# A mean's matmuls in a PSUM bank of their own, beside an open accumulation group (threshold attention and a feed-forward block, fp32)

## The chip, the cores and the metric

The kernel runs on one core of a Trainium2 chip. The metric is the device time of one execution in microseconds (us); the time before is the median of three runs, 1344.65 us (1344.35 to 1345.46). The profile is of one further execution. In it PE is TensorE's matmuls and PEld its weight loads, DVE is VectorE, ACT is ScalarE, POOL is GpSimd and SP the engine that issues most DMAs. Times inside the profile count from the start of its span.

## The reference

```python
# q, k, v: (8, 8, 576, 64) fp32; tau scalar
scores = scale * np.matmul(q, k.transpose(0, 1, 3, 2))
thresh = np.max(scores, axis=-1, keepdims=True) - tau
scores = np.where(scores >= thresh, scores, -1000000000.0)
attn = softmax(scores)                       # exp of scores - max, over its sum
x = matmul(attn, v), heads side by side      # (8, 576, 512)
mu = np.mean(x, axis=-1, keepdims=True)
var = np.mean((x - mu) ** 2, axis=-1, keepdims=True)
xn = (x - mu) / np.sqrt(var + 1e-06) * g_ln
out = x + np.maximum(xn @ w_ch1, 0.0) @ w_ch2   # w_ch1 (512, 2048), w_ch2 (2048, 512)
```

Softmax is written out in the reference; it is shortened here. All matrix work is in fp32.

## The kernel before

**Two streams.** The attention part goes through 72 steps, nine for each of the 8 batches (`SLOTS`). In a step PE makes scores, DVE takes the maxima, ACT the exponentials (L432), DVE the threshold and the sum (L439), POOL the division (L455); the weights are turned by DVE and two DMAs, and PE multiplies them with the values (L598, L608). The feed-forward part works on 16 groups of 288 tokens, two for each batch. `x` is held with features on the partitions, four slices of 128 features by 288 tokens.

**Order.** The order of the instructions on each engine is written out by hand (`manual_schedule`). Each step has four quarters. The feed-forward part of a group is a generator (`ffn_steps`): each `yield` hands back a kind and a cost, and `second_part` (L1035) lets it issue so many products in a quarter as a budget allows (`owed`). So PE's queue is a mixture of both streams, in a fixed order. A product (L96) is two matmuls of 64 output partitions each, and each of them stands in the trace as two weight loads and two matmuls, so a product is four of each.

**A group.** `mean_of` (L681) multiplies the sums over the four slices (`sums`, made by POOL at L650) with a constant matrix of 1/512 (`average`, L662), which leaves each token's mean on all partitions, tokens of the first half on partitions 0 to 63 and of the second on 64 to 127. `spread` then copies it with four ACT instructions (L674) into a tile in SBUF. `centre` (L691) subtracts it from the four slices of `x` with four DVE instructions (L698), which gives `xc`. `first_part` (L800) multiplies `xc` with w_ch1: 16 tiles of four products, each with a PSUM bank `p1`, emptied by ACT with the ReLU (L829). `second_quarters` (L871) multiplies the result with w_ch2 in seven segments of 16 products of 144 columns, instead of eight, with sums and differences of the weights prepared ahead (s2, s3, s4) and of the hidden values made on the way. Each segment (L903) accumulates in one PSUM bank `seg`, and ACT copies it out (L922). The seventh, with the weights s4 (kept in the tile `e`), is `p3`; the one before it is `p5`. The last group ends with `last_tiles` in place of the seventh segment.

**Banks.** Six of the eight PSUM banks hold scores. Two are left for all else (pool `ps_ff`, tag "ff", `bufs=2`): `p1`, `seg`, `mean` and, in the first steps, other tiles take them in turn. The framework orders engines by bank: an instruction that writes a bank waits until an instruction of another engine that was given that bank ahead of it is through, also where they touch other columns.

**The mean among the segments.** While the seven segments of a group are under way (`banks_taken`, L961), a mean that falls due for the next group is put on a list (`waiting_mean`). The seventh segment takes it up when its index d reaches 4 (`mean_from`): the mean is then put into columns 288 to 431 of the segment's own bank, with `start=False`, since the segment has opened the bank. A mean that falls due later than that, or while no segments run, takes a bank of its own (`start=True`). `centre` has to wait for the mean, and `first_part` of the next group for `xc`.

Of the kernel before, what the change touches and what calls it, by code (L numbers as in the profile page):

```python
# [8 lines left out]
F32 = mybir.dt.float32  # L9
# [9 lines left out]
def kernel(  # L19
# [41 lines left out]
    TOK = S // 2  # L61
# [14 lines left out]
    ps_ff = ctx.enter_context(tc.tile_pool(name="ps_ff", bufs=2, space=bass.MemoryType.PSUM))  # L76
# [19 lines left out]
    def product(out, lhsT, rhs, **flags):  # L96


        for h in range(2):
            r = slice(64 * h, 64 * h + 64)  # L100
            nc.tensor.matmul(out[r], lhsT=lhsT[:, r], rhs=rhs, **flags)  # L101
# [25 lines left out]
    def load_v(u):  # L127
# [21 lines left out]
        out=tau_sb, in_=bass.AP(tensor=tau.tensor, offset=tau.offset, ap=[[0, 128], [1, 1]])  # L149
# [5 lines left out]
    for t in v_rest:  # L155
# [9 lines left out]
        out=scl_sb, in0=tau_sb, scalar1=0.0, scalar2=SCALE, op0=ALU.is_ge, op1=ALU.mult  # L165
    )
    nc.vector.tensor_scalar(
        out=low_sb, in0=tau_sb, scalar1=0.0, scalar2=BIG, op0=ALU.is_lt, op1=ALU.mult
    )
    nc.vector.scalar_tensor_tensor(  # L170
        out=low_sb, in0=tau_sb, scalar=-1.0, in1=low_sb, op0=ALU.mult, op1=ALU.subtract
# [393 lines left out]
    groups, sums = {}, {}  # L565
# [89 lines left out]
    means, centred = {}, {}  # L655

    waiting_mean, banks_taken, among = [], [False], []

    HT = TOK // 2
    early, late = slice(0, HT), slice(HT, TOK)  # L660

    def average(to, bank, rhs, start, bias=None):  # L662


        for h in range(2):
            nc.tensor.matmul(
                bank[64 * h : 64 * h + 64], lhsT=avg_sb[:, 64 * h : 64 * h + 64],
                rhs=rhs[:, (early, late)[h]], start=start, stop=True, skip_group_check=True,
            )

        def spread():
            for at in range(2):
                for h in range(2):
                    nc.scalar.activation(  # L674
                        to[64 * at : 64 * at + 64, (early, late)[h]], bank[64 * h : 64 * h + 64],
                        func=AF.Identity, **({"bias": bias[64 * h : 64 * h + 64]} if bias is not None else {}),
                    )

        return spread

    def mean_of(g, bank=None):  # L681
        if bank is None and banks_taken[0]:
            waiting_mean.append(g)
            return
        start = bank is None
        if start:
            bank = ps_ff.tile([128, HT], F32, tag="ff", name="mean")
        means[g] = ffn.tile([128, TOK], F32, tag="mean", bufs=1, name="mean")
        average(means[g], bank, sums.pop(g), start)()

    def centre(g):  # L691
        nonlocal issued
# [14 lines left out]
    def drip(room=None, everything=False):  # L707


        urgent = [i for i, d in enumerate(drops) if d[0]]  # L710
        n = urgent[-1] + 1 if urgent else 0
        room = dict(room or {})
        while drops:
            _, when, eng, cost, go = drops[0]
            if n <= 0 and not everything:
                if when == now or room.get(eng, 0) < cost:
                    break
                room[eng] -= cost
            drops.pop(0)
            n -= 1  # L720
            go()
# [6 lines left out]
    def run_all(calls):  # L728
        now = calls[:]
        calls.clear()  # L730
        for fn in now:
            fn()
# [6 lines left out]
    def store(eng, g, m, o):  # L739
        ot = ffn.tile([128, TOK], F32, tag="o", bufs=4, name="ot")  # L740
        eng.transpose(ot, o)
        stores.append(lambda: send(g, m, ot))
# [27 lines left out]
    HD, HM = ND // 2, NK // 2  # L770
# [100 lines left out]
    def second_quarters(g, rb):  # L871
# [4 lines left out]
        s2, s3, s4 = more  # L876
        b11, b12 = hidden[:, :HD, early], hidden[:, :HD, late]
        b21, b22 = hidden[:, HD:, early], hidden[:, HD:, late]
# [21 lines left out]
                at = (slice(None), slice(d, d + 4))  # L900
                eng.tensor_tensor(out=out[at], in0=in0[at], in1=in1[at], op=op)  # L901

        def segment(weights, rhs, out=None, mean_from=HD):  # L903
            whole = ps_ff.tile([128, 512], F32, tag="ff", name="seg")
            bank = whole[:, :TOK].rearrange("p (m t) -> p m t", m=HM)
            for d in range(HD):
                if d == mean_from:
                    banks_taken[0] = False
                    while waiting_mean:
                        mean_of(waiting_mean.pop(0), whole[:, TOK : TOK + HT])  # L910
                        yield 2, 0
                for m in range(HM):
                    at, end = (d, m), (HD - 1, HM - 1)
                    product(
                        bank[:, m], lhsT=weights[:, m, d], rhs=rhs[:, d],
                        start=at == (0, 0), stop=at == end,
                    )
                    if at != end:
                        yield 2, 0.5
            if out is None:  # L920
                out = ffn.tile([128, HM, HT], F32, tag="part", bufs=4, name="part")
            nc.scalar.copy(out, bank)  # L922
            return out

        def last_tiles(weights, rhs):


            for m in range(HM):
                bank = ps_ff.tile([128, HT], F32, tag="ff", name="end")
                for d in range(HD):  # L930
                    product(
                        bank, lhsT=weights[:, m, d], rhs=rhs[:, d],
                        start=d == 0, stop=d == HD - 1,
                    )
                    if d < HD - 1:
                        yield 2, 0.5
                drip(everything=True)
                z = ffn.tile([128, HT], F32, tag="part", bufs=4, name="z")
                dve.tensor_tensor(out=z, in0=bank, in1=rb[:, late], op=ALU.mult)
                add(dve, y12[:, m], y12[:, m], z)  # L940
                store(dve, g, m, y[:, m])
                run_all(stores)
                if m < HM - 1:
                    yield 2, 0.5

        def add(eng, out, a, b):
            eng.tensor_tensor(out=out, in0=a, in1=b, op=ALU.add)
# [11 lines left out]
        ends_here = g == NG - 1  # L959
        later(("t3", 3, by_fours, pool, b12, b22, b12, ALU.subtract), urgent=pool)  # L960
        banks_taken[0] = True  # L961
        yield from segment(w2[0, 0], b11, y11)
        need("t3")
        later(("t2", 3, by_fours, dve, b11, b11, b12, ALU.add), urgent=dve)
        yield 2, 0.5
        p2 = yield from segment(w2[0, 1], b21)
        need("t2")
        later(("t4", 3, by_fours, pool, b21, b21, b11, ALU.subtract), urgent=pool)
        yield 2, 0.5
        p7 = yield from segment(s3, b12)  # L970
        yield 2, 0.5
        yield from segment(s2, b11, y12)
# [20 lines left out]
        else:  # L993
            later(("hi", 3, finish, pool, 1))
        yield 2, 0.5
        p3 = yield from last_tiles(s4, b22) if ends_here else segment(s4, b22, None, 4)
        if not ends_here:
            later(
                ("12", 1, add, dve, y12, y12, p3), ("done12", 2, finish, pool, 0, 1),
# [35 lines left out]
    def second_part(n, i):  # L1035

        nonlocal issued, owed, part, now
        part, now = i, QUARTERS * n + i
        if not queue:
            return  # L1040
        at = QUARTERS * n + i
        g = sum(issued >= e for e in ends)
        left = sum(ROOM[t % QUARTERS] for t in range(at, ready(g + 1))) if g + 1 < NG else 0
        owed += (ends[g] - issued) * ROOM[i] / left if left > 0 else 8


        steps = 0
        got = 1 if i in (0, QUARTERS - 1) else 2
        while queue and (owed >= 0.5 or got == 1 and i in (0, QUARTERS - 1)):
            got, cost = next(queue[0], (None, 0))  # L1050
            if got is None:
                queue.pop(0)
                got = 1
            elif got == 0:
                owed = 0.0
                break
            else:
                issued += cost
                owed -= cost
                steps += 1  # L1060
                if steps == 4 and among:
                    mean_of(among[0])
                    centre(among.pop())

    def group_ready(g):
        first = divmod(ready(g), QUARTERS)
        before = divmod(ready(g) - 1, QUARTERS) if g else first
        if g == 1:
            at_quarter(*before, lambda: among.append(g))
        else:  # L1070
            at_quarter(*before, mean_of, g)
            at_quarter(*(first if g and first[1] else before), centre, g)
        at_quarter(*first, lambda: queue.append(ffn_steps(g)))
# [4 lines left out]
    else:  # L1078
# [3 lines left out]
        for i in range(ND):  # L1082
            nc.sync.dma_start(
                out=w2_sb[:, :, i],
# [181 lines left out]
```

## Time and profile before

| what | value |
|---|---|
| median of 3 runs | 1344.65 us (1344.35 to 1345.46) |
| the profiled execution | 1344.68 us |
| its span, first to last instruction | 1342.9 us |
| granted TensorE clock, mean | 0.998 |
| chain that ended last, share of PE | 87% (DVE, ACT and POOL 3% each) |
| mean spreads at L674 (ACT), one instruction | 28 from a `seg` bank, median 285 ns; 36 from a `mean` bank, 284 ns |
| copy of a segment at L922 (ACT) | 399 ns |
| one `xc` subtraction at L698 (DVE) | median 451 ns |

A line of the groups reads: line, engine, operation, out<-in, partitions x elements, count; then busy time and mean ns of one; then the time that the engine stood idle just before them, and what ended most of it. A line of the timeline reads: start, duration, engine, line, operation, out<-in, count, and in brackets the idle time before it and what ended that. Matmuls overlap, so their own lengths are longer than the beat at which they follow each other: matmuls of 144 columns last 286 ns each and their pairs follow each other every 122 ns.

### The profile page before, as it was taken

Reading aid. Unit: us, or ns where it says so; the run is one execution under the profiler, and the core shown is the slowest. Engines: PE = TensorE matmul, PEld = TensorE weight load, DVE = VectorE, ACT = ScalarE, POOL = GpSimd, SP = SyncE. Lnnn points to the kernel's source line nnn. Section 1 sums busy time; section 2 is a strip of 40 time slices with the busy share of each in tenths; the row PEclk is TensorE's granted clock in tenths of the full one; section 3 lists DMA queues with packets and bytes.
Section 4 is the critical chain, followed back from the end, with each engine's and each line's share of the span. In section 5 each row is a group of like instructions: output and inputs, shape, how many; then the busy total and the mean of one; then the engine's idle time right before and its main releaser. Section 6 shows DMA issues by size and latency. Waiting matters only on the chain.

```text
span 1342.9 us, 40339 instructions
## 1 busy us (share of the span) xinstructions
PE 1305.7 (97%) x17304; PEld 985.6 (73%) x17304; DVE 874.0 (65%) x1544; ACT 490.7 (37%) x1107; POOL 628.1 (47%) x836
## 2 busy tenths in 40 slices
PE   8899899999999999999999999999999999999997
PEld 7665457769686786868778696877869687786957
DVE  7879886667666775666756677656766667665113
ACT  5866333242424333242333324233232323334130
POOL 3565556535445444444535454443444445344312
PEclk9999999999999999999999999999999999999999
DMA  8937874557643775447644576447764376444211
GB/s 167 295 102 183 204 187 156 178 155 195 176 150 120 194 203 158 151 156 191 174 151 151 165 179 191 143 143 192 194 178 152 120 197 185 129 152 133 85 19 20
DMA packets 335299, 213.93 MB, mean 159 GB/s; under 512 B 247376, under 2 KB 292688, under 8 KB 327056
## 3 DMA queue, kind: packets, MB, share of 16 engines
q1 hardware_dynamic: 329008, 210.46, 54.7%
q8 instruction: 136, 2.23, 0.7%
q10 hardware_dynamic: 5952, 0.74, 0.4%
q0 software_dynamic: 160, 0.15, 0.1%
q14 instruction: 43, 0.35, 0.1%
HBM read 124.00 MB, written 87.29 MB: 157 GB/s over the span
## 4 chain that ended last, share of the span: by engine, by line
PE 87%; DVE 3%; ACT 3%; POOL 3%; DMA 1%; issue 1%; SPq 1%; POOLq 0%; DVEq 0%; ACTq 0%
PE p L101 35%; PE seg L101 30%; PE sc L405 10%; PE sc L598 8%; PE sc L608 2%; DVE e L439 1%; ACT e L432 1%; POOL w L308 1%; ACT mean L674 1%; PE tp L101 1%; POOL e L455 1%; DMA qk_room<-in_k_dram 1%; SPq L118 1%; POOL hidden L844 0%; ACT em L489 0%
## 5 line engine op out<-in xcount | busy, mean ns | idle before, releaser
L101 PE MATMUL p<-xc,w 128*64 128x288 f32 x4096 | 519.8, 407 | 1.4 <-DVE xc L698 1.1
L101 PEld LDWEIGHTS p<-xc,w 128*64 128x64 f32 x4096 | 287.1, 137 | 204.8 <-issue 13.9
L419 DVE TENSOR_REDUCE neg<-sc 128x2 f32<-128x1152 f32 x144 | 188.9, 1352 | 256.6 <-PE sc L405 255.4
L455 POOL TENSOR_SCALAR e<-e,den 128x576 f32<-128x576 f32 x264 | 211.8, 814 | 133.6 <-DVE den L444 133.6
L101 PE MATMUL seg<-hidden,w 128*64 128x144 f32 x3840 | 247.9, 287 | 0.0
L101 PEld LDWEIGHTS seg<-hidden,w 128*64 128x64 f32 x3840 | 234.9, 137 | 11.5 <-issue 8.6
L439 DVE SCALAR_TENSOR_TENSOR e<-sc,thr,e 128x576 f32<-128x576 f32 x288 | 222.5, 810 | 20.2 <-POOL thr L423 11.6
L423 POOL TENSOR_SCALAR thr<-neg,low_sb 128x2 f32<-128x2 f32 x144 | 39.4, 274 | 378.8 <-DVE neg L419 376.4
L829 ACT ACTIVATE hidden<-p 128x288 f32<-128x288 f32 x256 | 106.4, 416 | 282.6 <-PE p L101 280.6
L432 ACT ACTIVATE e<-sc,neg 128x576 f32<-128x576 f32 x288 | 197.6, 753 | 2.6 <-DVE neg L419 2.5
L529 DVE STREAM_TRANSPOSE et<-e 128x1152 f32<-128x1152 f32 x118 | 161.1, 1372 | 14.5 <-POOL e L455 14.0
L405 PE MATMUL sc<-kT,qT 64*64 64x384 f32 (+3 forms) x2048 | 140.3, 403 | 2.8 <-DVE e L439 2.1
L598 PE MATMUL sc<-em,v_in 128*64 128x128 f32 (+1 forms) x2368 | 130.1, 263 | 2.7 <-DVE w L300 1.3
L598 PEld LDWEIGHTS sc<-em,v_in 128*64 128x64 f32 x2368 | 122.8, 137 | 11.6 <-DVE w L300 1.5
L101 PE MATMUL seg<-hidden,stage 128*64 128x144 f32 x1920 | 123.3, 286 | 0.0
L621 ACT COPY x<-sc 128x128 f32<-128x128 f32 x120 | 31.6, 266 | 245.7 <-PE sc L405 176.7
L101 PEld LDWEIGHTS seg<-hidden,stage 128*64 128x64 f32 x1920 | 117.6, 137 | 2.9 <-issue 2.9
L405 PEld LDWEIGHTS sc<-kT,qT 64*64 64x64 f32 x2048 | 76.3, 133 | 44.4 <-issue 21.4
L901 POOL TENSOR_TENSOR hidden<-hidden 128x576 f32<-128x576 f32 x60 | 84.8, 1428 | 50.7 <-ACT hidden L829 40.9
L922 ACT COPY part<-seg 128x288 f32<-128x288 f32 x74 | 29.9, 405 | 162.3 <-PE seg L101 162.1
L901 DVE TENSOR_TENSOR hidden<-hidden 128x576 f32<-128x576 f32 x60 | 50.3, 873 | 47.2 <-PE seg L101 44.2
L101 PE MATMUL seg<-hidden,e 128*64 128x144 f32 x896 | 60.4, 287 | 9.1 <-ACT mean L674 9.1
(134 smaller groups left out, 1069.5 us busy)
## 6 DMA issues: line engine op xcount, KB each, us to landing
scr<-et SPq DMA_DIRECT2D x63, 1152.0 KB, 5.0
em<-scr SPq DMA_DIRECT2D x63, 1024.0 KB, 5.7
out_dram<-ot SPq DMA_DIRECT2D x248, 36.0 KB, 3.7
q_in<-in_q_dram SPq DMA_DIRECT2D x120, 72.0 KB, 2.8
er<-scr SPq DMA_DIRECT2D x132, 64.0 KB, 5.2
k_in<-in_k_dram SPq DMA_DIRECT2D x116, 72.0 KB, 3.0
v_in<-in_v_dram SPq DMA_DIRECT2D x28, 256.0 KB, 5.4
w<-in_moe_w_ch_dram SPq DMA_DIRECT2D x10, 512.0 KB, 7.9
```

Of the source, the lines that this page charges most:

```text
L101: nc.tensor.matmul(out[r], lhsT=lhsT[:, r], rhs=rhs, **flags)
L405: nc.tensor.matmul(sc[h][64 * i : 64 * i + 64, at : at + n], lhsT=ql[r] if s == HP else qT[r, half, j * 128 + 64 * i : j * 128 + 64 * i + 64],
L419: nc.vector.tensor_reduce(out=neg[:, i], in_=pairs[h], axis=AXL.X, op=ALU.max, negate=True,)
L423: nc.gpsimd.tensor_scalar(out=thr[:, i], in0=neg[:, i], scalar1=-1.0, scalar2=low_sb, op0=ALU.mult, op1=ALU.add,)
L432: nc.scalar.activation(es[:, i], blocks[i], func=AF.Exp, bias=neg[:, i : i + 1])
L439: nc.vector.scalar_tensor_tensor(out=es[:, i], in0=blocks[i], scalar=thr[:, i : i + 1], in1=es[:, i], op0=ALU.is_ge, op1=ALU.mult, accum_o ...
L455: nc.gpsimd.tensor_scalar(out=es[:, i], in0=es[:, i], scalar1=den[:, i : i + 1], scalar2=1.0, op0=ALU.mult, op1=ALU.mult,)
L529: nc.vector.transpose(et[:, :, 64 * h : 64 * h + 64].rearrange("p n (j c) -> p j n c", j=2), es[:, 2 * h : 2 * h + 2].rearrange("p j (n c) ...
L598: nc.tensor.matmul(dst[64 * h : 64 * h + 64], lhsT=vt[:, h, c, :], rhs=pick(em[:, 2 * j : 2 * j + 2, c], h), start=c == 0 and first, stop= ...
L621: nc.scalar.copy(x_of(2 * b + (s > HP))[:, s % (HP + 1), 128 * j : 128 * j + 128], pv[j])
L829: nc.scalar.activation(hidden[:, d], p1, func=AF.Relu)
L901: eng.tensor_tensor(out=out[at], in0=in0[at], in1=in1[at], op=op)
```

## The change

The argument `mean_from` goes, and with it the mean inside the segment: a segment's bank holds the segment alone. The seventh segment is now stepped from outside. After eight of its steps the list of waiting means is worked off, and each mean takes a bank of its own, as the others do. After it a tile `passed` is taken from the same pool, which nothing writes or reads. Then the segment goes on. The words that come with the change say: "A group's mean in a bank of its own, four products sooner; the turn of the two free banks moved on by one, so that the next group's first tile takes it".

```diff
-    def mean_of(g, bank=None):
-        if bank is None and banks_taken[0]:
+    def mean_of(g):
+        if banks_taken[0]:
             waiting_mean.append(g)
             return
-        start = bank is None
-        if start:
-            bank = ps_ff.tile([128, HT], F32, tag="ff", name="mean")
+        bank = ps_ff.tile([128, HT], F32, tag="ff", name="mean")
         means[g] = ffn.tile([128, TOK], F32, tag="mean", bufs=1, name="mean")
-        average(means[g], bank, sums.pop(g), start)()
+        average(means[g], bank, sums.pop(g), True)()
...
-        def segment(weights, rhs, out=None, mean_from=HD):
-            whole = ps_ff.tile([128, 512], F32, tag="ff", name="seg")
-            bank = whole[:, :TOK].rearrange("p (m t) -> p m t", m=HM)
+        def segment(weights, rhs, out=None):
+            bank = ps_ff.tile([128, HM, HT], F32, tag="ff", name="seg")
             for d in range(HD):
-                if d == mean_from:
-                    banks_taken[0] = False
-                    while waiting_mean:
-                        mean_of(waiting_mean.pop(0), whole[:, TOK : TOK + HT])
-                        yield 2, 0
                 for m in range(HM):
...
-        p3 = yield from last_tiles(s4, b22) if ends_here else segment(s4, b22, None, 4)
+        last = last_tiles(s4, b22) if ends_here else segment(s4, b22)
+        for _ in range(8):
+            yield next(last)
+        banks_taken[0] = False
+        while waiting_mean:
+            mean_of(waiting_mean.pop(0))
+            ps_ff.tile([128, HT], F32, tag="ff", name="passed")
+        p3 = yield from last
```

## The prediction, made before the result was known

> **What bounds the kernel now.** I read the page first, then the waits of one batch, then the timeline of one pause. All times are us from the span's start.
>
> ```profile
> PE 1305.7 (97%) x17304; PEld 985.6 (73%) x17304; DVE 874.0 (65%) x1544; ACT 490.7 (37%) x1107; POOL 628.1 (47%) x836
> ...
> L101 PE MATMUL seg<-hidden,e 128*64 128x144 f32 x896 | 60.4, 287 | 9.1 <-ACT mean L674 9.1
> ```
>
> TensorE (PE) is busy 97% of the span and no other engine is over 65%. One row has idle time of PE of a kind that repeats: the products on `e` (the seventh segment, weights s4) waited 9.1 us for ACT at L674, which spreads the mean. The waits of PE in a whole batch, from 410 to 569, are this one line:
>
> ```profile
> PE seg L101 <- ACT mean L674: 1.3, 1, 1.3
> ```
>
> So within a batch PE stands still once, and what is saved there is not taken by another wait that is already there. The mean's tile view splits L674 into 28 spreads that read a seg bank and 36 that read a bank of their own. Four make one mean: seven groups (2, 4, ..., 14) have the shared bank, the other nine don't. Only those seven change. The timeline of the third of them:
>
> ```profile
> 566.70 0.77 ACT L432 ACTIVATE e<-sc,neg 128x576 f32<-128x576 f32 x1
> ...
> 567.33 0.43 ACT L922 COPY part<-seg 128x288 f32<-128x288 f32 x1
> 567.70 0.27 PEld L666 LDWEIGHTS seg<-sum,avg_sb 128*64 128x64 f32 x4
> ...
> 567.82 0.41 PE L666 MATMUL seg<-sum,avg_sb 128*64 128x144 f32 x4
> ...
> 568.31 1.17 ACT L674 ACTIVATE mean<-seg 64x144 f32<-64x144 f32 x4 [0.55 <-PE seg L666]
> ...
> 569.53 1.91 PEld L101 LDWEIGHTS seg<-hidden,e 128*64 128x64 f32 x32 [1.57 <-ACT mean L674]
> 569.53 2.18 PE L101 MATMUL seg<-hidden,e 128*64 128x144 f32 x32 [1.30 <-ACT mean L674]
> 569.59 0.17 DVE L444 RECIPROCAL den<-den 128x2 f32<-128x2 f32 x1
> 569.67 2.01 DVE L698 TENSOR_TENSOR xc<-x,mean 128x288 f32<-128x288 f32 x4
> 569.85 2.36 POOL L455 TENSOR_SCALAR e<-e,den 128x576 f32<-128x576 f32 x2 [0.20 <-DVE den L444]
> 571.42 0.27 PEld L101 LDWEIGHTS p<-xc,w 128*64 128x64 f32 x4
> 571.54 0.41 PE L101 MATMUL p<-xc,w 128*64 128x288 f32 x2
> ```
>
> After the mean's matmuls PE loads nothing until all four spreads are through, since the segment goes on in the bank they read. But see what follows: after the last product of the segment PE at once takes the next group's first tile, whose inputs xc DVE is still subtracting. The pause hides DVE's lateness. Groups 4 to 14 look alike to 0.02 us; group 2 differs (below).
>
> **The change, part by part.**
>
> *Place of the mean: nothing.* The words say four products sooner. In the diff, eight calls of next issue eight products; before, d reaches 4 after 4 x 2 products. In the trace 32 matmuls on `e` (four to a product) stand from 565.86 to the mean. The zero-cost yield that goes spends no budget, so the planner's order stays as it is. I take every engine's order as unchanged; only banks and waits differ.
>
> *The pause goes.* The mean's last load starts at 567.83 and loads follow each other by 0.122 in pairs, so the next would start at 567.945, its second pair at 568.067. They start at 569.533 and 569.588: 1.52 us lost on this pair's beat (the page's 1.3 counts from the modelled end of the mean's matmuls).
>
> *A new wait.* The mean now writes the bank of the fifth product p5 (the sixth segment), so it waits for p5's copy (L922), which stands behind exponentials in ACT's queue and ends at 567.76, 0.06 after the mean's first load. Behind the mean on PE stand the segment's last eight products and the next group; behind the mean on ACT nothing urgent. Nearest rows: a load starts 0.052 after the ACT work it waited for (569.481 to 569.533), and 0.077 after a separate wait of PE's sequencer (first mean, 74.59 to 74.66); such a sequencer wait stands 1.08 ahead of its load when it is free (group 3, 328.54 to 329.63). So the load starts at about 567.89, and since the second pair then follows by 0.055 and not 0.122, the beat loses 0.12. From below it is 0 (group 2, where the copy ends at 250.92 and the load is due at 251.39); from above 0.31, the gap of loads at the late wait at 323.2. I take 0.12. It moves the spread's end to 569.60; DVE started xc 0.032 after the spread in the last group (1276.167 to 1276.199), so xc could start at 569.63 and still starts at 569.67, when DVE is through with its reciprocal. Up to 0.16 the new wait costs xc nothing.
>
> *What is late next: xc.* Without it the first tile's matmuls would start at 571.545 - 1.52 + 0.12 = 570.14. The four subtractions start at 569.67, 570.02, 570.39 and 571.24 and take 0.44, 0.45, 0.92 and 0.45; they do not depend on PE. How PE follows DVE is shown by the last group:
>
> ```profile
> 1276.20 1.56 DVE L698 TENSOR_TENSOR xc<-x,mean 128x288 f32<-128x288 f32 x4 [2.64 <-ACT mean L674]
> ...
> 1276.71 0.20 PEld L101 LDWEIGHTS p<-xc,w 128*64 128x64 f32 x4 [0.56 <-DVE xc L698]
> ...
> 1277.08 1.04 PEld L101 LDWEIGHTS p<-xc,w 128*64 128x64 f32 x10 [0.17 <-DVE xc L698]
> ```
>
> The load is 0.054 behind the end of its subtraction, the matmul 0.05 behind the load, and a product takes 0.485. Product 1: xc ends 570.11, sequencer's wait 0.054 + 0.077, matmul at 570.29. Product 2: 570.77 (its xc at 570.48 is early). Product 3: PE is ready at 571.26, xc ends 571.31, so 571.42. Product 4: 571.90 (xc 571.68). The second tile starts at 572.39, before at 573.485: 1.10 saved.
>
> In group 2 ACT and PE come earlier against DVE: xc starts at 254.095 although the spread is through at 253.22. Its third subtraction ends at 255.74, so product 3 starts at 255.84 and the second tile at 256.81, before at 257.22: 0.41.
>
> *Sum:* 6 x 1.10 + 0.41 = 7.0 us. Downstream PE keeps it: DVE's next reduction idles 5.9 us for PE's scores, and the next transposed weights (em, fetched at 262.9 for use near 277.7) land 5.7 us after issue. The profiled execution took 1344.68 around a span of 1342.9, within 0.03 of the median, 1344.65, so the sum carries over: **1337.6 us**.
>
> *Two rules against it.* The trace grants PE a clock of 1.00 in the windows on both sides of the pause. In sentences that the sum does without: the Trainium skill, page "TensorE: Matmul & The Clock Gate", section "A second HAM failure mode: psum-queue depth-cycling", says that short idles of PE between groups that cycle through banks can make the clock swing between half and full. The change makes two or three short gaps of one; if each first tile (1.94 us) then ran at half clock, an estimate by that page is 7 x 1.94 = 13.6 us back, 1351. No run here shows it. The third subtraction takes 0.92 where the others take 0.45, while POOL scales e (569.85 to 572.2). If this stretch fell on the first subtraction, products 1 to 4 would follow each other from 570.76, the second tile would start at 572.70, and a group would save 0.79. The skill's page "SBUF — State Buffer", section "Who interferes with whom", has DVE and GpSimd shut each other out for a whole instruction; the row agrees in size.
>
> *The passed tile: nothing.* It holds no data. In the last group, whose mean had its own bank already, the first tile's loads began at 1276.71, while the copy of the segment ran from 1276.54 to 1276.94: so it was in the mean's bank, and I expect the same here.
>
> **The rivals.**
>
> 1. *The first tile gets the segment's bank* and waits for its copy. That copy ends at 572.24 - 1.40 = 570.84; product 1 then starts at 570.94 and the second tile at 572.88: 0.60 a group, 4.0 in all, **1340.6**. For it: the change meddles with the turn. Against: the last group.
> 2. *The words hold and the diff's count doesn't:* the mean stands four products (0.98 us) earlier, at 566.72, before p5's copy, and PE waits there 1.17 us. It keeps 0.35 in six groups and 0.4 in group 2: 2.5 us, **1342.1**. Against: the count.
> 3. *It doesn't do what it says:* the later products still wait for the spread through another dependency. **1344.6**. Against: in group 3 the mean has its own bank and the next loads (329.87) follow the mean's (329.63) on the beat.
> 4. *Slower: the mean comes late.* PE waits for p5's copy in order. If the mean is late by D, xc is late by D - 0.16, and the 1.10 is spent at D = 1.26. With the queue ahead to be refilled (1.08) and two more exponentials ahead of the copy (1.27), D = 2.35: 6 x 1.09 lost, 0.41 won in group 2, **1351**. Against: the copy misses by 0.06 only, ACT's order is unchanged, and late waits restarted after 0.08.
>
> Better than forecast is possible too: with a third subtraction of 0.45 the second tile would start at 570.29 + 4 x 0.485 = 572.23, 1.26 a group, and 0.57 in group 2 (254.71 + 1.94 against 257.22): 8.1 us, 1336.5. The ceiling is 7 x 1.52 = 10.6, 1334.0, but xc forbids it. With the new wait at 0.31, 0.15 goes in six groups: 1338.5.
>
> **How the numbers follow.** A measurement of this kernel can tell about 0.2%, 2.7 us, from no change. Forecast 0.72, its better form 0.02, rival 1 0.09: all faster by over 0.2%, 0.83. Rivals 2 (0.06) and 3 (0.06) are within it: 0.12. Rival 4: 0.05. The range runs from below the better form, 1335.5, to just past rival 1, 1341.3.
>
> **What would show it.** After: no row in which seg on `e` waits for ACT L674; all 64 spreads read a mean bank; a wait of about 0.2 us in front of the mean for ACT's copy in six groups; waits of PE for DVE xc of about 0.15 us on the first and third product, longer in group 2; and the means of even groups 157.0 apart and no longer 158.13. Wrong if the first tile waits for L922, if the mean's wait passes 0.3, or if the granted clock falls.

## The result, and the profile after

| | before | after |
|---|---|---|
| median | 1344.78 us (1344.35 to 1345.46, 6 runs) | 1338.44 us (1337.97 to 1339.2, 6 runs) |
| profiled execution, its span | 1344.68, 1342.9 us | 1338.63, 1336.8 us |
| from the first mean of group 1 to that of group 15 | 1106.47 us | 1100.04 us |
| one batch, group 7's mean to group 9's | 158.13 us | 157.03 us |

The changed kernel takes 0.9953 of the time before (95% interval 0.994 to 0.9966): 6.3 us less. The forecast was 1337.6, with 1335.5 to 1341.3 around it.

The page of the changed kernel, its busy line, its clock by slices, and the group of the first products on `xc` (busy time, mean ns, idle time before it and what ended that):

```profile
PE 1309.1 (98%) x17304; PEld 986.3 (74%) x17304; DVE 875.2 (65%) x1544; ACT 490.9 (37%) x1107; POOL 629.6 (47%) x836
...
PEclk9999999999999999999999999999999999999999
...
L101 PE MATMUL p<-xc,w 128*64 128x288 f32 x4096 | 521.9, 408 | 2.3 <-DVE xc L696 1.8
```

The row with 9.1 us of waiting for ACT at L674 has no successor: seg on `e` has 0.0 idle. Every engine has as many instructions as before. The mean granted clock is 0.997, before 0.998. The tile view of the mean (minimum, median and maximum ns, first and last start, form) now has one row for all spreads, from banks of their own, and the wait list of one batch (410 to 569; total us, times, longest) has a new entry:

```profile
L674 ACT ACTIVATE mean<-mean x64: 276/285/291, 76.5 to 1269.8; 64x144 f32<-64x144 f32 x64
```

```profile
PEld p L101 <- DVE xc L696: 1.1, 4, 0.5
```

So the pause for the spread is gone, and the products on `xc` wait in its place: four short waits of PE's weight loads in this batch, all in group 4, 1.1 us in all. The stretch around the mean of group 12, from the timeline of the changed kernel:

```profile
1037.82 0.43 ACT L914 COPY part<-seg 128x288 f32<-128x288 f32 x1
1038.31 0.20 PEld L666 LDWEIGHTS mean<-sum,avg_sb 128*64 128x64 f32 x4
...
1038.49 1.98 PEld L101 LDWEIGHTS seg<-hidden,e 128*64 128x64 f32 x32
...
1038.85 1.17 ACT L674 ACTIVATE mean<-mean 64x144 f32<-64x144 f32 x4 [0.59 <-PE mean L666]
...
1040.17 2.01 DVE L696 TENSOR_TENSOR xc<-x,mean 128x288 f32<-128x288 f32 x4
1040.35 2.36 POOL L455 TENSOR_SCALAR e<-e,den 128x576 f32<-128x576 f32 x2 [0.20 <-DVE den L444]
1040.66 0.20 PEld L101 LDWEIGHTS p<-xc,w 128*64 128x64 f32 x4 [0.19 <-DVE xc L696]
...
1040.86 0.40 ACT L914 COPY part<-seg 128x288 f32<-128x288 f32 x1 [0.84 <-PE seg L101]
1041.03 0.32 PEld L101 LDWEIGHTS p<-xc,w 128*64 128x64 f32 x4 [0.17 <-DVE xc L696]
...
1041.86 0.20 PEld L101 LDWEIGHTS p<-xc,w 128*64 128x64 f32 x4 [0.52 <-DVE xc L696]
```

Read it downwards. The mean's load stands 0.05 behind the end of the fifth product's copy (1038.257 to 1038.309). The segment's loads follow the mean's on the beat (1038.49), while ACT still spreads. DVE starts `xc` at 1040.17, 0.15 behind the end of the spread (1040.02), since its reciprocal comes first, and the first product's load follows the first subtraction by 0.054 (1040.605 to 1040.659). The third product waits longest: the third subtraction takes 0.916, the others 0.437 to 0.450. And the first tile's load at 1040.66 starts before the segment's copy (1040.86) has begun, so the tile isn't in the segment's bank.

### The profile page after: what moved, and what is told of

Read it like the earlier page. It is cut to its first block, busy times and chain, and to the rows that moved or that the text cites. A ratio compares the mean times of both kernels' runs of the same rounds, so it can differ in the third digit from the quotient of the medians.

```text
span 1336.8 us, 40333 instructions
## 1 busy us (share of the span) xinstructions
PE 1309.1 (98%) x17304; PEld 986.3 (74%) x17304; DVE 875.2 (65%) x1544; ACT 490.9 (37%) x1107; POOL 629.6 (47%) x836
## 4 chain that ended last, share of the span: by engine, by line
PE 87%; POOL 3%; DVE 3%; ACT 2%; issue 1%; DMA 1%; SPq 0%; POOLq 0%; DVEq 0%; ACTq 0%
PE p L101 35%; PE seg L101 30%; PE sc L405 10%; PE sc L598 8%; PE sc L608 2%; DVE e L439 1%; POOL w L308 1%; ACT e L432 1%; PE tp L101 1%; POOL e L455 1%; DMA em<-scr 1%; POOL hidden L842 0%; ACT em L489 0%; DMA scr<-et 0%; POOL stage L795 0%
```

## The experiments

"Batch" below is the distance of the means of groups 7 and 9, and "seven groups" the distance of the means of groups 1 and 15, both in the profiled execution. They leave out the start-up, in which the first mean of group 1 stands anywhere from 167.40 to 169.72 in these ten traces whatever was changed.

| kernel | median us | ratio to before (95%) | batch | seven groups |
|---|---|---|---|---|
| before | 1345.79 and 1345.25 | | 158.13 | 1106.47 |
| after | 1338.44 | 0.9953 (0.994 to 0.9966) | 157.03 | 1100.04 |
| no_passed | 1338.63 | 0.9948 (0.9936 to 0.9961) | 157.03 | 1100.04 |
| first_tile_in_seg_bank | 1341.28 | 0.9971 (0.996 to 0.9982) | 157.55 | 1102.63 |
| mean_after_4 | 1342.55 | 0.9974 (0.9965 to 0.9983) | 157.63 | 1103.06 |
| mean_after_12 | 1343.91 | 0.9987 (0.9979 to 0.9996) | 157.87 | 1105.07 |
| values_first | 1335.11 | 0.9921 (0.9908 to 0.9935) | 156.67 | 1096.29 |
| values_first_shared_bank | 1345.57 | 1.0001 (0.9992 to 1.001) | 158.14 | 1106.55 |
| xc_between_halves | 1336.05 | 0.9929 (0.9915 to 0.9942) | 156.71 | 1096.69 |
| shared_bank_after_12 | 1346.12 | 1.0009 (1.0 to 1.0018) | 158.13 | 1106.92 |

The first four experiments (no_passed to mean_after_12) were timed on one chip and the last four on another, each beside the kernel before (the two medians in its row); after has its own pair, in the section on the result.

**Does the turn of the banks do anything?** The theory says that the passed tile moves nothing.

```diff
-            ps_ff.tile([128, HT], F32, tag="ff", name="passed")
```

> The changed kernel without the tile that nothing uses. Theory (the saving comes from the bank alone, the rest of the 1.52 us pause being given back to late xc): the pool hands out a bank when a tile is first used, so the unused tile moves nothing, the next group's first tile still takes the mean's bank, and the time stays at 1338.4 within 0.5. Rival (the turn matters): without it the first tile falls into the segment's bank and waits for its copy, about 2.5 to 4 us more, 1341 to 1342.5.

The batch is 157.03 with and without it, and the seven groups differ by less than 0.01. The passed tile does nothing. What it is said to do can be done for real: a small matmul into the passed tile, and another after the first tile's first product, hold the bank, so that the first tile must take the segment's. Their values are used nowhere.

```diff
+    def touch(t):
+        nc.tensor.matmul(t[:64, :32], lhsT=avg_sb[:, :64], rhs=ident[:, :32], start=True, stop=True)
...
+                while held:
+                    touch(held.pop())
...
         p3 = yield from last
+        if pass_on:
+            held.append(ps_ff.tile([128, HT], F32, tag="ff", name="passed"))
+            touch(held[0])
```

> The changed kernel with the turn forced the other way: after the seventh segment a tile takes the mean's bank and is written by a matmul of 32 columns before and after the next group's first product (its values are used nowhere), so that the first tile takes the segment's bank. Theory: the first tile of the even groups waits for the segment's copy, which ends 0.6 us after the first tile's start in the changed kernel; with the waits for xc that are then covered, 0.4 us a group in groups 4 to 14 and nothing in group 2, plus about 0.1 us a group for the small matmuls: 2.5 to 4 us, 1341 to 1342.5. Rival (which bank the first tile has does not matter, since xc is late anyway): 1338.4 to 1339.

The timeline of this kernel in group 12:

```profile
1041.83 2.01 DVE L699 TENSOR_TENSOR xc<-x,mean 128x288 f32<-128x288 f32 x4
...
1042.11 0.26 PEld L660 LDWEIGHTS passed<-ident,avg_sb 128*64 128x64 f32 x2
...
1042.53 0.40 ACT L919 COPY part<-seg 128x288 f32<-128x288 f32 x1 [0.84 <-PE seg L101]
1042.98 0.20 PEld L101 LDWEIGHTS p<-xc,w 128*64 128x64 f32 x4 [0.60 <-ACT part L919]
```

Now the first load waits for the copy: it starts at 1042.98, 0.71 behind the end of the first subtraction (1042.271), where in after it was 0.054. A batch costs 0.53 more than after. The small matmuls have a small part in it, about 0.06: with one of them between, the second product follows the first by 0.543, and by 0.536 in after, and the third follows the second by 0.535, where a product with nothing to wait for takes 0.485. It is what the first rival would have looked like (0.60 saved a group predicted, 158.13 - 157.55 = 0.58 here), and it shows that after isn't that.

**Where should the mean stand?** The words put it four products sooner, the diff doesn't. These two kernels move it for real, to four and to twelve products.

```diff
-        for _ in range(8):
+        for _ in range(4):
```

> The changed kernel with the mean truly four products sooner, after the fourth product of the seventh segment. Theory: the mean's matmuls then wait for the copy of the sixth segment, which ends when it did; PE idles some 1.1 us there and has four more products to do after it, so the first tile starts 0.7 us later in groups 4 to 14, nothing in group 2: 4 us, 1342.4 (1341 to 1343.5). Rival (sooner is better, because xc is what is late): xc comes sooner and 1 to 3 us are saved, 1335.5 to 1337.5.

```profile
1040.35 0.43 ACT L914 COPY part<-seg 128x288 f32<-128x288 f32 x1
...
1040.83 0.20 PEld L666 LDWEIGHTS mean<-sum,avg_sb 128*64 128x64 f32 x4 [1.07 <-ACT part L914]
...
1042.69 1.64 DVE L696 TENSOR_TENSOR xc<-x,mean 128x288 f32<-128x288 f32 x3
...
1043.95 0.14 PEld L101 LDWEIGHTS p<-xc,w 128*64 128x64 f32 x2
```

At four products PE stands still for the fifth product's copy, 1.07 us, and the first tile (last line, no bracket) then finds `xc` ready: the wait has moved from behind the mean to in front of it. 0.50 of the 1.10 a batch is left.

```diff
-        for _ in range(8):
+        for _ in range(12):
```

> The changed kernel with the mean four products later, after the twelfth product; in the odd groups too, where the list is then still open when the mean falls due. Theory: the spread and xc come 0.9 us later, and the first tile, which waits for xc already, starts 0.6 to 1.1 us later in groups 4 to 14: 3.5 to 6.5 us, 1342 to 1345; the pause itself stays away, since the bank is the mean's own. Rival (the saving is the mean's place among the products, and any place with a bank of its own keeps it): 1338.4 within 1.

```profile
1041.56 0.27 PEld L666 LDWEIGHTS mean<-sum,avg_sb 128*64 128x64 f32 x4
...
1042.17 1.17 ACT L674 ACTIVATE mean<-mean 64x144 f32<-64x144 f32 x4 [1.53 <-PE mean L666]
...
1043.37 2.03 DVE L696 TENSOR_TENSOR xc<-x,mean 128x288 f32<-128x288 f32 x4 [0.74 <-ACT mean L674]
1043.88 0.20 PEld L101 LDWEIGHTS p<-xc,w 128*64 128x64 f32 x4 [1.08 <-DVE xc L696]
```

At twelve the copy is no longer in the way, but the spread ends late (1043.34), DVE waits 0.74 for it, and PE 1.08 for DVE. 0.26 a batch is left. Between the copy on one side and the spread on the other, eight is the best of the three.

**Is the given-back part `xc`?** If the first tile's lateness is what keeps a batch from the full pause, then work that needs no `xc`, put in front of that tile, must bring it back; and the same move must bring nothing in the kernel before, where the pause hides DVE. In both kernels 32 matmuls of an earlier block's values, each with its weight load, go ahead of the first tile of the even groups.

```diff
+        run_all(ahead_of_tiles)
...
+        if n + 1 > SLOTS and (n + 1) % SLOTS == HP + 2:
+            at_quarter(n + 1, 1, ahead_of_tiles.append, go)
+            at_quarter(n + 1, 3, run_all, ahead_of_tiles)
```

> The changed kernel with one more edit: in the step in which an even group begins, the 32 matmul pairs of the values (1.9 us of PE) are issued between the seventh segment and the next group's first tile, and not eleven products into it. Theory (what is left of the pause is xc, and nothing else holds the first tile): PE works through the values while DVE subtracts, the waits for xc go, 0.45 us a group in groups 4 to 14 and 1.1 in group 2: 1334.6 (1333.8 to 1336). Rival (PE is held by something that comes later in any case, or the values then wait for their banks): 1338.4 or more.

```profile
1034.43 0.20 PEld L666 LDWEIGHTS mean<-sum,avg_sb 128*64 128x64 f32 x4
...
1036.29 2.01 DVE L696 TENSOR_TENSOR xc<-x,mean 128x288 f32<-128x288 f32 x4
...
1036.57 1.79 PEld L598 LDWEIGHTS sc<-em,v_in 128*64 128x64 f32 x32
...
1038.33 1.22 PEld L101 LDWEIGHTS p<-xc,w 128*64 128x64 f32 x12
```

The subtractions (1036.29 to 1038.30) now lie beside the values (from 1036.57), and the first product's loads, at 1038.33, wait for nothing. A batch is 156.67.

> The kernel before, with the mean still in the segment's bank, and the same edit of the values' place. Theory: the pause lies inside the segment, ahead of the values, and xc was not late, so nothing is won: 1345 to 1345.8, as before. Rival (the pause is only what PE would have waited for xc anyway, and filling that place wins it back without a bank of its own): 1336 to 1340.

```profile
1043.34 1.18 ACT L674 ACTIVATE mean<-seg 64x144 f32<-64x144 f32 x4 [0.54 <-PE seg L666]
...
1044.57 1.91 PEld L101 LDWEIGHTS seg<-hidden,e 128*64 128x64 f32 x32 [1.57 <-ACT mean L674]
...
1044.71 2.01 DVE L698 TENSOR_TENSOR xc<-x,mean 128x288 f32<-128x288 f32 x4
...
1046.46 1.79 PEld L598 LDWEIGHTS sc<-em,v_in 128*64 128x64 f32 x32
```

With the shared bank the pause of 1.57 stands as it was, and the batch is 158.14. The same move is worth 0.36 a batch with the mean in its own bank (0.45 was expected) and nothing without: the two waits stand one behind the other, and the second only shows when the first is gone.

The other way to the same end is to let DVE subtract sooner: in the even groups `xc` runs between the two halves of the block's weights, after the first of their two reciprocals.

```diff
     def weights(...)
+            if i == 1:
+                run(n, "mid")
...
-            at_quarter(*(first if g and first[1] else before), centre, g)
+            at_quarter(first[0], "mid", centre, g) if g and first[1] == 2 else at_quarter(*before, centre, g)
```

> The changed kernel with the four subtractions of an even group moved forward on DVE, to between the second and the third of the step's four threshold operations, so that DVE waits for the spread there and the subtractions fall between POOL's two stretches of scaling. Theory: the third subtraction then takes 0.45 and not 0.92, xc starts 0.1 us sooner, the second tile starts 0.3 us sooner in groups 4 to 14 and 1 us in group 2, and the 3 us by which DVE's own chain is late are covered, since DVE idles 5.9 us before the next reduction: 1335.4 (1334.5 to 1337). Rival (DVE's lateness comes back at the next scores or the next transposed weights): 1338.4 to 1342.

```profile
1035.93 1.17 ACT L676 ACTIVATE mean<-mean 64x144 f32<-64x144 f32 x4 [0.59 <-PE mean L668]
1037.13 1.56 DVE L698 TENSOR_TENSOR xc<-x,mean 128x288 f32<-128x288 f32 x4 [1.48 <-ACT mean L676]
...
1037.64 0.20 PEld L101 LDWEIGHTS p<-xc,w 128*64 128x64 f32 x4
...
1038.02 2.01 PEld L101 LDWEIGHTS p<-xc,w 128*64 128x64 f32 x18 [0.17 <-DVE xc L698]
```

DVE now stands idle for 1.48 us, which costs nothing, and the four subtractions take 1.56 in place of 2.01 (0.457, 0.452, 0.451, 0.452): the third no longer takes 0.92. One short wait is left, for the second subtraction (last line): the second product follows the first by 0.536 and not 0.485. A batch is 156.71.

**Is a later mean enough without the new bank?** The kernel before, with its mean moved to twelve products:

```diff
-        p3 = yield from last_tiles(s4, b22) if ends_here else segment(s4, b22, None, 4)
+        p3 = yield from last_tiles(s4, b22) if ends_here else segment(s4, b22, None, 6)
```

> The kernel before with the mean after the twelfth product of the segment instead of the eighth, still in its bank. Theory: the pause is the spread's length and waits for nothing but the spread, wherever the mean stands, 1.5 us a group; xc comes 1 us later and just meets the first tile: 1344.5 to 1346. Rival (the place of the mean sets the pause): a place four products later costs or wins more than 2 us.

```profile
1044.09 1.17 ACT L674 ACTIVATE mean<-seg 64x144 f32<-64x144 f32 x4 [1.53 <-PE seg L666]
...
1045.30 2.03 DVE L698 TENSOR_TENSOR xc<-x,mean 128x288 f32<-128x288 f32 x4 [0.74 <-ACT mean L674]
1045.32 0.93 PEld L101 LDWEIGHTS seg<-hidden,e 128*64 128x64 f32 x16 [1.57 <-ACT mean L674]
```

In the even groups the pause is the same 1.57 after eight products and after twelve, and `xc`, 0.74 later, is still hidden: four products follow the pause, and its end releases both. The batch stays at 158.13. The median is 0.12 over the upper end of what was expected. The trace shows 0.44 more over the seven groups, all of it in group 2 (162.12 between the means of groups 1 and 3, before 161.69), and an eighth pause, 1.54 by the loads, behind the mean of group 15.

That mean of group 15 points at something else that this kernel changes. With the list open for longer, the means of the odd groups fall into the segment's bank too: 56 of the 64 spreads read a `seg` bank, before 28. Group 3:

```profile
330.52 0.30 PEld L666 LDWEIGHTS seg<-sum,avg_sb 128*64 128x64 f32 x4
330.76 1.82 PEld L598 LDWEIGHTS sc<-em,v_in 128*64 128x64 f32 x32
331.12 1.17 ACT L674 ACTIVATE mean<-seg 64x144 f32<-64x144 f32 x4 [2.79 <-PE seg L666]
332.52 1.02 PEld L101 LDWEIGHTS seg<-hidden,e 128*64 128x64 f32 x16
```

Here 32 matmuls of the values stand between the mean and the rest of the segment. The spread (331.12 to 332.29) is through before PE comes back to the shared bank at 332.52, and PE doesn't stop: the batch, which holds an even and an odd group, is no longer than before. In group 15 nothing stands between, and PE stops. So sharing the bank costs a pause only where PE's next work is in that bank.

## Why the prediction was right

*Place of the mean, and order.* PE's 17304 loads stand in the same order in both traces, but for two neighbours in the start-up (at 37 us), and the mean has eight products ahead of it in both. Right: the words don't describe the diff. mean_after_4 shows what the words would have given, 1106.47 - 1103.06 = 3.41 us over the seven groups, against the 2.5 of the second rival (0.50 a group where it had 0.35, since the wait for the copy takes 1.02 from PE's beat and not 1.17).

*The pause.* 1.52 on the pair's beat in groups 4 to 14 of before. With `xc` out of the way in two different manners a batch gains 1.47 (values_first) and 1.43 (xc_between_halves). That is the pause less what is still waited for: 0.05 for the new wait in values_first (1.52 - 0.05 = 1.47), and in xc_between_halves 0.04 for it and 0.05 at the second product (1.52 - 0.04 - 0.05 = 1.43). Right, and shown from both sides.

*The new wait.* Predicted 0.12 in six groups, measured 0.04 in five. In groups 4, 8, 10, 12 and 14 the mean's load comes 0.227 behind the one before it, where 0.116 would be the beat, so it is 0.11 late. But the mean's second pair follows by 0.055 and not 0.122, and the segment's next pair (1038.486 in group 12) stands only 0.04 behind the beat. The prediction made the load 0.19 late, with a wait of PE's sequencer (0.077) in front of it that the trace doesn't have. The sum doesn't feel the difference, since PE waits for `xc` behind it. In group 2 there is none, as predicted; in group 6 none either, since ACT was ahead of PE there.

*What is late next.* Predicted: products 1 and 3 wait for `xc`, the third because its subtraction takes 0.92, and 1.10 a group is left. Measured 1.107 on average in groups 4, 8, 10, 12 and 14; in group 2 0.43, predicted 0.41. That it fits to 0.01 is partly luck, since two small errors cancel. What counts is product 3, which waits for its subtraction whatever went before. The prediction put its first matmul 0.11 behind the end of the third subtraction; it stands 0.055 behind it (1041.808 to 1041.863). But after a wait the next product came 0.536 later in place of 0.485, so that the second tile starts 1.08 behind the third subtraction in both. The first product's matmul was 0.12 sooner than predicted (1040.661 - 1040.605 = 0.056, predicted 0.18), which is lost again in front of product 3.

*Collision of DVE and POOL.* The third subtraction takes 0.92 in groups 2, 4 and 12 of after, and 0.451 in group 12 of xc_between_halves, where POOL's scaling is through (1037.22) before the second subtraction begins. The Trainium skill, page "SBUF — State Buffer", section "Who interferes with whom", calls the port pair that DVE and GpSimd share an exclusive lock, and says that a DVE instruction with two SBUF inputs contends with a GpSimd instruction that reads SBUF. The prediction's row "agrees in size" only in part: two subtractions beside a running scaling took 0.437 and 0.450, and the long ones in these ten traces were all ones in which an instruction of POOL ended (below).

*The clock.* With four gaps of 0.17 to 0.52 us in most of the even groups (up to 0.64 in group 6 and 0.97 in group 2) the granted clock is 0.997, and 0.996 to 0.998 in the profiled executions of all experiments. The Trainium skill, page "TensorE: Matmul & The Clock Gate", section "A second HAM failure mode: psum-queue depth-cycling", tells of a clock that swings when PE idles briefly between groups of matmuls; no run here shows it.

*The sum.* This is the step that was mis-sized: 7.0 predicted, 6.1 between the two profiled executions and 6.3 between the medians. Over the seven groups it is 1106.47 - 1100.04 = 6.43; the rest is the start-up, 0.32 later in this execution of after. Against 7.0 that is 0.57 too little, and group 6 alone lacks 0.63: 157.66 and not 157.03 from mean to mean, so it saves 0.47 where 1.10 was predicted. (The idle 5.9 us that the prediction gives for DVE's next reduction is another reduction's; those behind the subtractions of groups 2, 4 and 6 idle 6.4, 7.1 and 7.1, which only widens the margin.) The larger part of the 0.63 is in the scores ahead of group 6's mean. First the timeline of before, then of after, PE's loads of the same stretch:

```profile
561.01 0.21 PEld L405 LDWEIGHTS sc<-kT,qT 64*64 64x64 f32 x8
...
561.71 1.02 PEld L405 LDWEIGHTS sc<-kT,qT 64*64 64x64 f32 x20 [0.17 <-issue]
...
563.11 0.93 PEld L101 LDWEIGHTS seg<-hidden,w 128*64 128x64 f32 x16 [0.39 <-issue]
```

```profile
559.79 0.21 PEld L405 LDWEIGHTS sc<-kT,qT 64*64 64x64 f32 x8
...
560.50 0.47 PEld L405 LDWEIGHTS sc<-kT,qT 64*64 64x64 f32 x11 [0.17 <-issue]
561.26 0.67 PEld L405 LDWEIGHTS sc<-kT,qT 64*64 64x64 f32 x9 [0.29 <-issue]
...
562.32 0.81 PEld L101 LDWEIGHTS seg<-hidden,w 128*64 128x64 f32 x14 [0.38 <-issue]
```

From the first load to the segment's it is 2.10 before and 2.53 after: 0.43 lost, in a gap after the eleventh of twenty loads, in the middle of a set of four that belong together. The other 0.20 is at `xc`: in this group POOL's scaling starts 0.06 ahead of the subtractions (568.66 and 568.72) and not 0.18 behind, they take 0.459, 0.918, 0.444 and 0.909, and PE waits for the second and the fourth. no_passed has the same gap at the same load (0.426 and 0.427) and the same 157.66; in the other seven experiments no batch from group 3 on differs from its neighbours. The place in PE's program alone can't be the cause: xc_between_halves issues the same loads in the same order there, and this one comes 0.006 behind the load before it. No transfer of the DMA queue that loads instructions falls into the gap in either trace. Its cause stays open.

*The rivals.* The first, second and third are out by the traces (first load ahead of the segment's copy; eight products; no wait for L674). The fourth needs a mean late by over 1.26, and its load was 0.11 late; mean_after_12 shows how it would have come: by the rival's rule a mean four products (0.98) late costs 0.98 - 0.16 = 0.82 a group, and measured is 157.87 - 157.03 = 0.84.

## What to carry to other kernels

A bank that an open sum shares with something that must be read stops the sum for as long as the reads take, here four at 0.285 us and their latencies, 1.52 a time. That costs time only where PE has nothing else to do in between: the odd groups of shared_bank_after_12 share a bank at no cost, behind 32 matmuls of other work. A bank of its own removes the pause only as far as the next input is ready. So look, before counting the pause as gain, at which engine used the pause to catch up: its lateness is the price, here 0.3 of 1.4 us, and moving independent work in front of the late input (values_first, 0.9921 of before, the lowest median here) or the late work forward (xc_between_halves, 0.9929) brings it back. The first of these moves brings nothing without the change (values_first_shared_bank); the second wasn't run without it.

## What the runs showed of the hardware

- In group 12 of after, a load that waited for DVE or ACT started 0.05 behind the end of what it waited for (0.052 behind the copy, 0.054 behind the subtraction), with no separate wait of PE's sequencer in front of it, in contrast to the first mean of the kernel (0.077 behind such a wait, in before).
- A late load doesn't cost its whole lateness: the mean's load came 0.11 late, the next pair closed up to 0.055 behind it, and the segment's loads behind them were 0.04 late.
- A subtraction of 128x288 took 0.44 to 0.46 us, also beside a scaling that began and went on. In all the long ones an instruction of POOL ended: 0.916 (1040.892 to 1041.808; a scaling ends at 1041.504), 0.918 and 0.909 in group 6 (scalings end at 569.707 and 570.908), 1.054 in group 1 (172.477 to 173.531; POOL's addition ends at 173.22). Not every such ending goes with a long one: in xc_between_halves a scaling ends at 1037.223, 0.09 into the first subtraction, which takes 0.457. The scaling takes 0.74 alone and mostly 1.05 to 1.28 beside the subtractions, so it may be POOL that stood still while the short ones ran. No run separates the two engines' shares.
- PE's loads stopped for 0.43 us in the middle of a set of four, at the same load in two kernels (after and no_passed), with nothing in the trace that they waited for. A third kernel with the same loads in the same order didn't stop there.
- The start-up, up to group 1's mean, varied by 2.3 us between the ten traces (167.40 to 169.72), though what the edits move stands behind that mark; the seven groups behind it repeated to within 0.01 us between after and no_passed. A difference of a few us is read better between two marks in the trace than from whole times.
